# Loading PE weights once for two matmuls, and letting ACT end the kernel, in a decode step with a 64K cache

## The chip, the cores and the metric

One core of one Trainium2 chip. The metric is the device time of one execution in microseconds (us); medians of repeated executions are quoted.

Terms: PE is the matmul engine, PEld its weight loads (LDWEIGHTS), DVE the vector engine, ACT the scalar engine, POOL the general engine, SP the engine that issues most DMAs. "DMA engine" is one of the 16 that move data for a core. A "landing" is the moment at which a transfer's last data is reported. "Warm" and "cold" are PE at a granted clock of 1.00 and of 0.50.

## The reference, cut to what matters

One token (B = Sq = 1) passes through a grouped-query attention with a 65,536-position cache, and through a small gated MLP; the two are mixed by a sigmoid gate.

```python
q = (x @ wq).reshape(1, 1, 32, 128)                   # wq 1024 x 4096
scores = einsum('bhqd,bhkd->bhqk', q, k) * 128**-0.5  # 4 kv heads, 8 q heads on each
o = einsum('bhqk,bhkd->bhqd', softmax(scores), v)
a = o.reshape(1, 1, 4096) @ wo                        # wo 4096 x 1024
b = gated_mlp(x, w_in, w_sp, b_sp, w_out)             # w_in 1024 x 3584, w_out 1792 x 1024
return g * a + (1 - g) * b                            # g = sigmoid(sum(x * gate_w))
```

K and V are 64 MiB each in bf16. With the weights the kernel reads 162 MB for one token, and every byte is used once.

## The kernel before

All big inputs pass through four buffers of 32 KB per partition (4 MB each), in one queue issued by SP. A buffer is loaded again when its last reader is done.

```python
kv = ctx.enter_context(tc.tile_pool(name="kv", bufs=4))
def load(src, shape, name):
    t = kv.tile([P, CT * P], BF16, name=name, tag="kv")      # 128 partitions x 32 KB
    ...
    nc.sync.dma_start(out=v, in_=src)
```

A K tile is transposed on DVE in four quarters, and each quarter is multiplied by 128 columns that hold the queries. The two values of `k` use the same weights, but each `nc.tensor.matmul` brings its own load:

```python
for v in range(VC):                                    # VC = 4 quarters
    nc.vector.transpose(out=kt[:].bitcast(I32), in_=kb[:, v * n:(v + 1) * n])
    ...
    for b in range(BP):                                # BP = 4
        for k in range(2):
            nc.tensor.matmul(s_ps[:, k * HN:(k + 1) * HN],       # 512 columns
                lhsT=wt[g % 2][:, v, b]..., rhs=kx[:, b // 2, b % 2, ...], ...)
```

The second product (probabilities times V) uses 32 columns of the PE array at a time, so that four matmuls stand side by side in the array:

```python
for c in range(CC):                                    # CC = 32
    t = c % NB                                         # NB = 4 column groups of 32
    nc.tensor.matmul(o_ps[g][t * B:(t + 1) * B, :], lhsT=ptt[g, j][:, c, :],
                     rhs=vx[:, c], ...)                # 128 x 512
```

The end: the last tile is `wo`, in pieces of 16, 8, 4, 2, 1 and 1 rows per partition. After each piece `project` multiplies what has come, and the result goes out:

```python
nc.vector.tensor_copy(out=out_sb[:], in_=out_ps[:])
nc.sync.dma_start(out=out..., in_=out_sb[::B, :])
```

## Time and profile before

| | before |
|---|---|
| time, median (lowest to highest) | 386.87 us (386.82 to 386.92) |
| span of the profiled execution | 385.2 us |
| queue of inputs (q1) | 162.01 MB, 98.1% of the time of 16 engines |
| PE, PE loads, DVE busy | 55%, 23%, 54% |

Lines of the page of the kernel before: the span; busy us, share of the span and count of instructions of each engine; and of three DMA queues packets, MB, and the share of 16 engines' span that their packets took.

```profile
span 385.2 us, 3265 instructions
...
PE 212.4 (55%) x1396; PEld 89.7 (23%) x1396; DVE 209.2 (54%) x207; ACT 39.2 (10%) x54; POOL 4.4 (1%) x10
...
q1 hardware_dynamic: 6200, 162.01, 98.1%
q8 instruction: 11, 0.18, 0.2%
q14 instruction: 4, 0.03, 0.0%
```

The input queue fills the DMA engines; nothing else comes near. The queues q8 and q14 look like nothing: they fetch instructions, 0.2% in all.

The groups that the change is about (line, engine, operation, tiles, shapes, count | busy us, mean ns of one | idle before, releaser):

```profile
L301 PE MATMUL s_ps<-kt,wt 128*128 128x512 bf16 x512 | 139.0, 426 | 88.4 <-DVE kt L295 87.2
...
L301 PEld LDWEIGHTS <-wt 128*128 128x128 bf16 x512 | 52.6, 105 | 173.5 <-DVE kt L295 72.8
L344 PE MATMUL o_ps<-vt,pt 128*32 128x512 bf16 x512 | 39.4, 457 | 15.4 <-DMA vt<-in_A_v_cache_dram 15.4
...
L344 PEld LDWEIGHTS <-pt 128*32 128x32 bf16 x512 | 15.9, 109 | 34.9 <-issue 27.1
```

Each of the two products has 512 matmuls and 512 loads. In steady state, from the timeline (start us, duration us):

```profile
205.55 1.90 PE L301 MATMUL s_ps<-kt,wt 128*128 128x512 bf16 x8 [0.29 <-DVE kt L295]
...
207.38 1.91 PE L344 MATMUL o_ps<-vt,pt 128*32 128x512 bf16 x32
```

Eight score matmuls take 1.90 us, 0.24 us each. The 32 matmuls of a whole V tile take 1.91 us, 0.06 us each, as four run side by side. And the first half of an x projection, at the start:

```profile
12.24 3.18 PE L190 MATMUL z_ps<-win_t,xT 128*32 128x448 bf16 x32
```

The end of the chain of waits (start us, duration us, what):

```profile
347.38 34.34 DMA wo_t<-in_A_wo_dram
...
381.76 0.43 PE out_ps L382 x4
...
382.22 0.42 DVE out_sb L421
```

The last `wo` piece is issued at 347.4 us and has landed at 381.72; then come 0.43 us of matmul, 0.42 us of copy, and the store. So the kernel ends about 3.5 us after its last input byte is reported.

Windows of half a microsecond there (window, length, busy time and count of PE, PEld, DVE, ACT, POOL, the PE clock granted, DMA share, GB/s):

```profile
379.50:380.00 0.50, 0.33 (x14) 0.14 (x5) 0.00 (x0) 0.00 (x0) 0.00 (x0) 1.00 0.19 70
380.00:380.50 0.50, 0.04 (x4) 0.04 (x7) 0.00 (x0) 0.00 (x0) 0.00 (x0) 1.00 0.24 82
380.50:381.00 0.50, 0.36 (x8) 0.17 (x8) 0.00 (x0) 0.00 (x0) 0.00 (x0) 1.00 0.13 49
```

The share is 0.19, 0.24 and 0.13.

### The profile page before, as it was taken

The numbers are of one execution on the slowest core, as the hardware profiler recorded it, in microseconds if no ns is written. First come the engines' busy times: TensorE is split into PE (matmuls) and PEld (weight loads), VectorE is DVE, ScalarE is ACT, GpSimd is POOL, SyncE is SP. The second block draws the span as 40 slices with busy tenths as digits, with TensorE's granted clock in tenths as the row PEclk, the third lists the DMA queues.
The fourth block names the chain that finished last, engine by engine and source line by source line (L and its number), as shares of the span: only waits on it lengthen the run. The fifth ranks groups of instructions, "written<-read, shape, count | busy, mean of one in ns | idle before, by whom it ended". The sixth has DMA issues, their size and how long they took to land.

```text
span 385.2 us, 3265 instructions
## 1 busy us (share of the span) xinstructions
PE 212.4 (55%) x1396; PEld 89.7 (23%) x1396; DVE 209.2 (54%) x207; ACT 39.2 (10%) x54; POOL 4.4 (1%) x10
## 2 busy tenths in 40 slices
PE   0433447775377656464876474637773837663352
PEld 0111113232222212122322121222221312331141
DVE  5141288996697372757864636569646456510010
ACT  1010001111601101014011010140110101400000
POOL 4000000000000000000000000000000000000000
PEclk9966559999779969695699695977895958565558
DMA  8999999999999999999999999999999999999993
GB/s 334 429 436 434 436 433 432 436 431 435 432 429 427 429 419 434 432 432 436 434 436 429 434 429 433 422 436 427 425 432 430 436 436 436 427 429 430 427 408 149
DMA packets 6251, 162.23 MB, mean 421 GB/s; under 512 B 728, under 2 KB 732, under 8 KB 1116
## 3 DMA queue, kind: packets, MB, share of 16 engines
q1 hardware_dynamic: 6200, 162.01, 98.1%
q8 instruction: 11, 0.18, 0.2%
q14 instruction: 4, 0.03, 0.0%
q10 hardware_dynamic: 36, 0.00, 0.0%
HBM read 162.01 MB, written 0.00 MB: 421 GB/s over the span
## 4 chain that ended last, share of the span: by engine, by line
DMA 65%; DVE 18%; PE 9%; issue 5%; ACT 1%; SPq 0%; ACTq 0%; DVEq 0%
DMA kn<-in_A_k_cache_dram 44%; DVE kt L295 15%; DMA vt<-in_A_v_cache_dram 9%; DMA wo_t<-in_A_wo_dram 9%; PE s_ps L301 6%; DMA wb<-in_B_b_sp_dram 2%; DVE pt L335 1%; PE o_ps L344 1%; PE z_ps L190 1%; ACT sc L310 1%; PE om_ps L355 0%; SPq L417 0%; ACT sc L332 0%; DVE mx L314 0%; DVE mx L297 0%
## 5 line engine op out<-in xcount | busy, mean ns | idle before, releaser
L301 PE MATMUL s_ps<-kt,wt 128*128 128x512 bf16 x512 | 139.0, 426 | 88.4 <-DVE kt L295 87.2
L295 DVE STREAM_TRANSPOSE kt<-kn 128x2048 int32<-128x2048 int32 x64 | 143.3, 2283 | 68.4 <-DMA kn<-in_A_k_cache_dram 68.4
L301 PEld LDWEIGHTS <-wt 128*128 128x128 bf16 x512 | 52.6, 105 | 173.5 <-DVE kt L295 72.8
L344 PE MATMUL o_ps<-vt,pt 128*32 128x512 bf16 x512 | 39.4, 457 | 15.4 <-DMA vt<-in_A_v_cache_dram 15.4
L310 ACT CAST sc<-s_ps 128x1024 bf16<-128x1024 f32 x16 | 16.2, 1013 | 254.9 <-PE s_ps L301 254.9
L344 PEld LDWEIGHTS <-pt 128*32 128x32 bf16 x512 | 15.9, 109 | 34.9 <-issue 27.1
L335 DVE STREAM_TRANSPOSE pt<-sc 128x1024 bf16<-128x1024 bf16 x16 | 18.6, 1217 | 6.8 <-ACT sc L332 6.8
L332 ACT ACTIVATE sc<-sc,nb 128x1024 bf16<-128x1024 bf16 x16 | 18.2, 1136 | 9.5 <-DVE nb L328 9.5
L352 DVE COPY o_sb<-o_ps 128x512 f32<-128x512 f32 x4 | 2.6, 662 | 27.2 <-PE o_ps L344 27.2
L297 DVE TENSOR_REDUCE mx<-sc 128x1 f32<-128x1024 bf16 x12 | 14.3, 1188 | 1.2 <-ACT sc L310 1.1
L355 PE MATMUL om_ps<-o_sb,pick 128*32 128x128 f32 x32 | 7.7, 421 | 13.1 <-DVE o_sb L352 13.1
L190 PE MATMUL q_ps<-wq_t,xT 128*32 128x512 bf16 x64 | 7.1, 623 | 9.1 <-DMA wq_t<-in_A_wq_dram 9.1
L314 DVE TENSOR_REDUCE mx<-sc 128x1 f32<-128x1024 bf16 x4 | 4.9, 1220 | 12.3 <-ACT sc L310 12.3
L382 PE MATMUL out_ps<-wo_t,oa 128*32 128x256 bf16 x128 | 6.0, 334 | 7.7 <-DMA wo_t<-in_A_wo_dram 7.7
L190 PEld LDWEIGHTS <-xT 128*32 128x32 bf16 x128 | 5.2, 140 | 20.5 <-issue 20.5
L355 PEld LDWEIGHTS om_ps<-o_sb,pick 128*32 128x32 f32 x32 | 5.0, 168 | 17.2 <-DVE o_sb L352 16.3
L254 DVE TENSOR_TENSOR rowt<-q_ps,own_b 128x512 f32<-128x512 f32 x2 | 1.3, 685 | 14.1 <-PE q_ps L190 14.1
L190 PE MATMUL z_ps<-win_t,xT 128*32 128x448 bf16 x64 | 6.2, 567 | 4.8 <-DMA win_t<-in_B_w_in_dram 4.8
L421 DVE CAST out_sb<-out_ps 128x256 bf16<-128x256 f32 x1 | 0.4, 425 | 12.4 <-PE out_ps L382 12.4
L318 PE MATMUL mt_ps<-ident_f,m 128*1 128x128 f32 x4 | 1.2, 296 | 10.2 <-DVE m L316 10.2
L382 PEld LDWEIGHTS <-oa 128*32 128x32 bf16 x128 | 4.4, 116 | 9.1 <-issue 7.2
L202 DVE TENSOR_TENSOR rowt<-z_ps,own_b 128x448 f32<-128x448 f32 x2 | 1.2, 620 | 9.3 <-PE z_ps L190 9.3
(86 smaller groups left out, 57.4 us busy)
## 6 DMA issues: line engine op xcount, KB each, us to landing
kn<-in_A_k_cache_dram SPq DMA_DIRECT2D x16, 4096.0 KB, 27.1
vt<-in_A_v_cache_dram SPq DMA_DIRECT2D x16, 4096.0 KB, 34.6
wq_t<-in_A_wq_dram SPq DMA_DIRECT2D x2, 4096.0 KB, 28.3
win_t<-in_B_w_in_dram SPq DMA_DIRECT2D x2, 3584.0 KB, 15.0
wo_t<-in_A_wo_dram SPq DMA_DIRECT2D x1, 4096.0 KB, 31.1
wout_t<-in_B_w_out_dram SPq DMA_DIRECT2D x1, 3584.0 KB
wo_t<-in_A_wo_dram SPq DMA_DIRECT2D x1, 2048.0 KB
wo_t<-in_A_wo_dram SPq DMA_DIRECT2D x1, 1024.0 KB
```

Of the source, the lines that this page charges most:

```text
L190: nc.tensor.matmul(ps[t * B:(t + 1) * B, k * HN:k * HN + n], lhsT=xT[:, i * KH + c:i * KH + c + 1].to_broadcast([P, B]), rhs=w[:, c, o:o + ...
L295: nc.vector.transpose(out=kt[:].bitcast(I32), in_=kb[:, v * n:(v + 1) * n])
L297: nc.vector.reduce_max(**late.pop())
L301: nc.tensor.matmul(s_ps[:, k * HN:(k + 1) * HN], lhsT=wt[g % 2][:, v, b].rearrange("p a v h -> p (a v h)"), rhs=kx[:, b // 2, b % 2, k * C ...
L310: nc.scalar.copy(out=sct[g, j][:], in_=s_ps[:])
L314: nc.vector.reduce_max(**late.pop())
L332: nc.scalar.activation(out=sct[g, j][:], in_=sct[g, j][:], func=ACT.Exp, scale=SCALE, bias=nb[:, 0:1], accum_out=lss[g][:, j:j + 1])
L335: nc.vector.transpose(out=ptt[g, j][:].rearrange("p c x -> p (c x)"), in_=sct[g, j][:])
L344: nc.tensor.matmul(o_ps[g][t * B:(t + 1) * B, :], lhsT=ptt[g, j][:, c, :], rhs=vx[:, c], start=(j == 0 and c < NB), stop=(j == NT - 1 and ...
L352: nc.vector.tensor_copy(out=o_sb[:], in_=o_ps[g][:])
L355: nc.tensor.matmul(om_ps[gs, :], lhsT=pick[:, i * REP:(i + 1) * REP, :].rearrange("p h q -> p (h q)"), rhs=o_sb[:, i * DH:(i + 1) * DH], s ...
L382: nc.tensor.matmul(out_ps[t * B:(t + 1) * B, :], lhsT=vec[:, c0 + c:c0 + c + 1].to_broadcast([P, B]), rhs=w[:, c, t * NO:(t + 1) * NO], st ...
```

## The change

Its intent: take PE's repeated weight loads out. The second matmul of a pair keeps the weights of the first, and a hook deletes its LDWEIGHTS from the finished program. For the second product that means pairs of chunks as 64 columns (two matmuls with the same 64 columns; half of each result is of use), which gives a larger `o_ps` and another `head_out`. ACT does the last copy and the store.

```diff
+    def drop_repeated_loads(n):        # run on the finished program
+        ...                            # deletes the LDWEIGHTS of each matmul marked by same_weights()
+    nc.at_finalize(drop_repeated_loads)
 ...                                    # x projections: t outside, k inside
-                    nc.tensor.matmul(
+                    ins = nc.tensor.matmul(
                         ps[t * B:(t + 1) * B, k * HN:k * HN + n],
 ...
+                    if k > 0:
+                        same_weights(ins)
 ...                                    # scores: the same two lines
     def v_tile(g, j, vt):
-            o_ps[g] = pso.tile([P, VC * DH], FP32, name="o_ps")
+            o_ps[g] = pso.tile([P, 2, VC * DH], FP32, name="o_ps")
-        for c in range(CC):
-            t = c % NB
-            nc.tensor.matmul(o_ps[g][t * B:(t + 1) * B, :], lhsT=ptt[g, j][:, c, :], rhs=vx[:, c], ...)
+        for u in range(CC // 2):
+            hs = slice(u % 2 * P // 2, (u % 2 + 1) * P // 2)
+            for e in range(2):
+                ins = nc.tensor.matmul(o_ps[g][hs, e, :],
+                    lhsT=ptt[g, j][:, 2 * u:2 * u + 2, :].rearrange("p c x -> p (c x)"),
+                    rhs=vx[:, 2 * u + e], ...)
+                if e > 0:
+                    same_weights(ins)
     def head_out(g):                    # copy and 4 matmuls become a masked product, a sum and 1 matmul
 ...
-    nc.vector.tensor_copy(out=out_sb[:], in_=out_ps[:])
-    nc.sync.dma_start(out=out..., in_=out_sb[::B, :])
+    nc.scalar.copy(out=out_sb[:], in_=out_ps[:])
+    nc.scalar.dma_start(out=out..., in_=out_sb[::B, :])
```

One effect is not in the diff's lines: tiles were removed, added and resized ahead of the four big buffers, so these moved by 544 bytes in each partition (43,968 to 44,512, by the addresses in the two built programs).

More of the change, by code (lines that the diff above doesn't have):

```diff
@@ L73, with same_weights @@
     pss = ctx.enter_context(tc.tile_pool(name="pss", bufs=2, space=bass.MemoryType.PSUM))
-    psm = ctx.enter_context(tc.tile_pool(name="psm", bufs=2, space=bass.MemoryType.PSUM))
+    psm = ctx.enter_context(tc.tile_pool(name="psm", bufs=1, space=bass.MemoryType.PSUM))
     pso = ctx.enter_context(tc.tile_pool(name="pso", bufs=1, space=bass.MemoryType.PSUM))
     psl = ctx.enter_context(tc.tile_pool(name="psl", bufs=1, space=bass.MemoryType.PSUM))
+    held = set()
+    def same_weights(ins):
+        held.add(ins.ins.name)
+    def drop_repeated_loads(n):
+        for block in n.main_func.blocks:
+            drop, load_at = [], None
+            for i, ins in enumerate(block.instructions):
+                kind = type(ins).__name__
+                if kind == "InstLdweights":
+                    load_at = i if ins.sync_info is None else None
+                elif kind == "InstMatmult":
+                    if ins.name in held and load_at is not None:
+                        drop.append(load_at)
+                    load_at = None
+            for i in reversed(drop):
+                del block.instructions[i]
+    nc.at_finalize(drop_repeated_loads)
     def load(src, shape, name):
@@ L121 @@
         nc.gpsimd.memset(t[:], 0.0)
-    pbits = const.tile([P, 5], I32, name="pbits")
+    pbits = const.tile([P, 6], I32, name="pbits")
     for i, m in enumerate((P // KC - 1, B - 1, QD - 1, REP - 1)):
@@ L128 @@
                             scalar2=None, op0=ALU.logical_shift_right)
-    pf = const.tile([P, 6], FP32, name="pf")
+    nc.vector.tensor_scalar(out=pbits[:, 5:6], in0=pidx[:], scalar1=REP.bit_length() - 1,
+                            scalar2=2 * VC - 1, op0=ALU.logical_shift_right, op1=ALU.bitwise_and)
+    pf = const.tile([P, 7], FP32, name="pf")
     nc.vector.tensor_copy(out=pf[:, 0:1], in_=pidx[:])
-    nc.vector.tensor_copy(out=pf[:, 1:6], in_=pbits[:])
+    nc.vector.tensor_copy(out=pf[:, 1:7], in_=pbits[:])
     def one_hot(shape, dtype, in0, col, name):
@@ L178 @@
     nc.vector.tensor_copy(out=own_bb[:], in_=own_b[:].unsqueeze(1).to_broadcast([P, NB, B]))
-    pick = one_hot([P, B, QD], FP32, row[:, :B].unsqueeze(2).to_broadcast([P, B, QD]), 2, "pick")
+    own_8 = one_hot([P, 2 * VC], FP32, row[:, :2 * VC], 6, "own_8")
     own_q = one_hot([P, QD], FP32, row[:, :QD], 3, "own_q")
@@ L186, in x_rows @@
         for c in range(KH):
-            for k in range(F // (NB * ZN) if n == ZN else NHB):
-                for t in range(NB):
+            for t in range(NB):
+                for k in range(F // (NB * ZN) if n == ZN else NHB):
                     o = (k * NB + t) * n
-                    nc.tensor.matmul(
+                    ins = nc.tensor.matmul(
                         ps[t * B:(t + 1) * B, k * HN:k * HN + n],
@@ L300, in k_tile @@
                 for k in range(2):
-                    nc.tensor.matmul(
+                    ins = nc.tensor.matmul(
                         s_ps[:, k * HN:(k + 1) * HN],
@@ L306, in k_tile @@
                         skip_group_check=True)
+                    if k > 0:
+                        same_weights(ins)
         if j == 0:
@@ L339, in v_tile @@
         if j == 0:
-            o_ps[g] = pso.tile([P, VC * DH], FP32, name="o_ps")
+            o_ps[g] = pso.tile([P, 2, VC * DH], FP32, name="o_ps")
         vx = vt.rearrange("p (v c d) -> p c v d", v=VC, d=DH)
-        for c in range(CC):
-            t = c % NB
-            nc.tensor.matmul(
-                o_ps[g][t * B:(t + 1) * B, :], lhsT=ptt[g, j][:, c, :], rhs=vx[:, c],
-                start=(j == 0 and c < NB), stop=(j == NT - 1 and c >= CC - NB),
-                skip_group_check=True)
+        for u in range(CC // 2):
+            hs = slice(u % 2 * P // 2, (u % 2 + 1) * P // 2)
+            for e in range(2):
+                ins = nc.tensor.matmul(
+                    o_ps[g][hs, e, :],
+                    lhsT=ptt[g, j][:, 2 * u:2 * u + 2, :].rearrange("p c x -> p (c x)"),
+                    rhs=vx[:, 2 * u + e], start=(j == 0 and u < 2),
+                    stop=(j == NT - 1 and u >= CC // 2 - 2), skip_group_check=True)
+                if e > 0:
+                    same_weights(ins)
@@ L349, in head_out @@
     def head_out(g):
         gs = slice(g * B, (g + 1) * B)
-        o_sb = wk.tile([P, VC * DH], FP32, name="o_sb")
-        nc.vector.tensor_copy(out=o_sb[:], in_=o_ps[g][:])
-        om_ps = psm.tile([P, DH], FP32, name="om_ps", tag="m")
-        for i in range(VC):
-            nc.tensor.matmul(
-                om_ps[gs, :],
-                lhsT=pick[:, i * REP:(i + 1) * REP, :].rearrange("p h q -> p (h q)"),
-                rhs=o_sb[:, i * DH:(i + 1) * DH], start=(i == 0), stop=(i == VC - 1),
-                skip_group_check=True)
@@ L360, in head_out @@
-        ls_ps = psm.tile([P, NT], FP32, name="ls_ps", tag="m")
-        nc.tensor.matmul(ls_ps[gs, :], lhsT=hsel[:].rearrange("p h q -> p (h q)"),
-                         rhs=lss[g][:], start=True, stop=True, skip_group_check=True)
+        om8 = big.tile([P, 2 * VC, DH], FP32, name="om8")
+        nc.vector.tensor_tensor(
+            out=om8[:], in0=o_ps[g][:].rearrange("p e (v d) -> p (e v) d", d=DH),
+            in1=own_8[:].unsqueeze(2).to_broadcast([P, 2 * VC, DH]), op=ALU.mult)
+        o_sb = wk.tile([P, DH], FP32, name="o_sb")
@@ new lines, in head_out @@
+        nc.vector.tensor_reduce(out=o_sb[:], in_=om8[:].rearrange("p x d -> p d x"), axis=AX.X,
+                                op=ALU.add)
+        om_ps = psm.tile([P, DH + NT], FP32, name="om_ps", tag="m")
+        hs = hsel[:].rearrange("p h q -> p (h q)")
+        nc.tensor.matmul(om_ps[gs, DH:], lhsT=hs, rhs=lss[g][:], start=True, stop=True,
+                         skip_group_check=True)
+        nc.tensor.matmul(om_ps[gs, :DH], lhsT=hs, rhs=o_sb[:], start=True, stop=True,
+                         skip_group_check=True)
@@ L363, in head_out @@
         rl = wk.tile([P, 2], FP32, name="rl")
-        nc.vector.reduce_sum(out=rl[gs, 0:1], in_=ls_ps[gs, :], axis=AX.X)
+        nc.vector.reduce_sum(out=rl[gs, 0:1], in_=om_ps[gs, DH:], axis=AX.X)
         nc.vector.reciprocal(out=rl[gs, 1:2], in_=rl[gs, 0:1])
@@ L367, in head_out @@
         nc.vector.tensor_tensor(
-            out=om[gs], in0=om_ps[gs, :].rearrange("p (q c) -> p q c", c=OC),
+            out=om[gs], in0=om_ps[gs, :DH].rearrange("p (q c) -> p q c", c=OC),
             in1=own_q[gs, :].unsqueeze(2).to_broadcast([B, QD, OC]), op=ALU.mult)
@@ L420 @@
     out_sb = const.tile([P, NO], BF16, name="out_sb")
-    nc.vector.tensor_copy(out=out_sb[:], in_=out_ps[:])
-    nc.sync.dma_start(out=out.rearrange("o t (q n) -> (o t q) n", n=NO), in_=out_sb[::B, :])
+    nc.scalar.copy(out=out_sb[:], in_=out_ps[:])
+    nc.scalar.dma_start(out=out.rearrange("o t (q n) -> (o t q) n", n=NO), in_=out_sb[::B, :])
     last = {}
```

## The prediction

> **What bounds the kernel.** The input stream. The DMA queue table gives 162.01 MB in queue q1, whose packets fill 98.1% of the 16 engines' span; the slice row stays near 427 to 436 GB/s. The Trainium skill ("DMA: Bandwidth & Descriptors", Specifications) names 435 GB/s as the fabric ceiling; this trace agrees (436 in the best slices). 162.01 MB at the middle's 431 GB/s is 376 of 385.2 us (estimate). The rest is about 2.5 us before the first bytes and 5 us after the stream thins out (in the windows the DMA share falls to 0.2 at 379.5 us). PE is busy 55%, its loads 23%, DVE 54%. By the issue times against bytes moved, the queue always holds 9 to 35 us of issued work, least near 115 us: a buffer freed a few us earlier or later changes nothing.
>
> **What the change does.**
> 1. Scores: 256 of 512 loads go. A warm quarter of a K tile (8 matmuls) takes 1.90 us; I guess 0.22 to 0.23 per matmul after, for 0.24. PE busy there falls from 139 to 125–135 us. The quarters are paced by the 2.28 us transposes on DVE, these by the DMA: off the path.
> 2. Second product: before, four 32-column matmuls run side by side (32 in 1.91 us warm, 3.60 cold). After, 64 columns leave two places, and the two matmuls of a pair use the same one, so on average two run at once: 3.8 us warm, 5.5–7 cold (estimate, double). Loads fall from 512 to 256, but matmul busy rises from 39 to about 75 us: worse for PE. There is room: a K and V pair costs PE about 10 + 3.8 us, and its stream takes 19.4.
> 3. x projections: also two side by side instead of four; a half goes from 3.0–3.6 to 5.5–7 us. The q chain starts 2–3 us later; the first K transpose (50.9 us) slips by 0.5–2 us. The backlog absorbs it.
> 4. head_out: a 0.69 us copy and 1.9 us of matmuls become two DVE operations of about 1.2 us (estimate from the 128x1024 reduction, 1.22 us) and 0.5 us of matmul: +0.3 us.
> 5. End: ACT copies (about 0.38 us, estimate from 1013 ns for 1024 columns and 171 ns for one) where DVE took 0.425, and issues the store itself: 0.1 us and one hop saved.
>
> **On the critical path.** Only 5, and perhaps 2 and 4 in the tail. The last V tile lands at 362.08 us; oa was ready at 369.8, the first wo tile lands at 371.8. After: oa at 372–373, some us later if the pairs do not overlap. The projection of the first wo tile (3.2 us) then ends near 376, before the second wo piece (376.7), and even a few us more are caught up before the last piece at 381.7, which still ends the kernel.
>
> **Predicted:** 386.6 us, 80% range 386.0 to 387.2. Faster by over 2%: 0.01; within 2%: 0.97; slower by over 2%: 0.02.
>
> **What would show it.** Queue share near 98%, mean about 421 GB/s; loads fall from 1396 to about 800, their busy time to about half; o_ps matmul busy nearly doubles (last V tile 5.5–7 us); DVE waits longer for kn; the last wo piece lands near 381.7; the chain of waits is still mostly DMA.
>
> **What would make it wrong.** Pairs that do not overlap, so that head_out ends after 376 us and the catch-up fails (up to +2 us); a starved queue near 115 us, seen as a slice clearly below 420 GB/s; a slow start of the store on ACT (+0.3 us); a DMA rate that shifts with the buffers' places.

## The result and the profile after

| | before | after |
|---|---|---|
| time, median of 4 runs | 386.89 us | 385.80 us (385.71 to 385.88) |
| span of the profiled execution | 385.2 us | 383.9 us |
| last `wo` piece landed | 381.72 us | 380.64 us |
| instruction fetches on q8 | 11 | 8 |

The ratio is 0.9971 (95% interval 0.9953 to 0.9988). Ratios here are the mean time of one kernel's fast runs over that of the other's of the same rounds, so they are not quite the ratios of the medians. The gain is 1.1 us where 0.3 was predicted, and the time lies below the stated range.

The page after:

```profile
span 383.9 us, 2650 instructions
...
PE 242.3 (63%) x1372; PEld 59.3 (15%) x796; DVE 218.5 (57%) x211; ACT 39.6 (10%) x55; POOL 4.4 (1%) x10
...
q1 hardware_dynamic: 6192, 162.01, 98.5%
q8 instruction: 8, 0.13, 0.1%
```

The loads fall to 796 and PEld from 89.7 to 59.3 us. PE busy rises. The bytes are the same. q8 has 8 fetches for 11. The groups of the two products in the changed kernel (256 loads each, for 512):

```profile
L326 PE MATMUL s_ps<-kt,wt 128*128 128x512 bf16 x512 | 142.3, 437 | 67.9 <-DVE kt L320 67.3
...
L372 PE MATMUL o_ps<-vt,pt 128*64 128x512 bf16 x512 | 69.2, 432 | 8.8 <-DMA vt<-in_A_v_cache_dram 8.8
L326 PEld LDWEIGHTS <-wt 128*128 128x128 bf16 x256 | 27.6, 108 | 184.0 <-issue 122.9
...
L372 PEld LDWEIGHTS <-pt 128*64 128x64 bf16 x256 | 17.2, 124 | 57.9 <-issue 56.4
```

The same eight score matmuls and the same V tile in the timeline of the changed kernel:

```profile
205.67 1.89 PE L326 MATMUL s_ps<-kt,wt 128*128 128x512 bf16 x8 [0.30 <-DVE kt L320]
...
207.49 3.65 PE L372 MATMUL o_ps<-vt,pt 128*64 128x512 bf16 x32
```

And its first half projection, with k inside and t outside:

```profile
12.30 3.18 PE L213 MATMUL z_ps<-win_t,xT 128*32 128x448 bf16 x32
```

Eight score matmuls take 1.89 us with half of their loads gone, for 1.90: the loads had been hidden. A V tile takes 3.65 us instead of 1.91: with 64 columns only two matmuls run side by side. For PE the change is a loss. The half projection takes 3.18 us in either order.

The end of its chain of waits:

```profile
349.05 31.60 DMA wo_t<-in_A_wo_dram
...
380.69 0.32 PE out_ps L414 x4
...
381.02 0.37 ACT out_sb L453
```

And its windows of half a microsecond:

```profile
379.50:380.00 0.50, 0.27 (x8) 0.07 (x1) 0.00 (x0) 0.00 (x0) 0.00 (x0) 1.00 0.45 168
380.00:380.50 0.50, 0.29 (x4) 0.10 (x4) 0.00 (x0) 0.00 (x0) 0.00 (x0) 1.00 0.04 12
380.50:381.00 0.50, 0.29 (x4) 0.10 (x3) 0.00 (x0) 0.00 (x0) 0.00 (x0) 1.00 0.00 0
```

In the same windows the share is 0.45 and then 0.04 and 0: more engines work at 379.5 us than before, and by 380.5 all are done.

From the landing of the last piece to the end of the span it is now 3.28 us (383.92 - 380.64, the span with two decimals), for 3.45 before (385.17 - 381.72): 0.17 us less, with the shorter last matmul group (0.32 us for 0.43, at a granted clock of 1.00 in the last window shown; before, it was 0.67 from 381 to 382 us) and ACT's copy (0.37 for 0.42). The other 1.08 us lie ahead of the landing: the same 162.01 MB arrived earlier. No step of the prediction had a reason for that.

### Where the 1.08 us are: the slowest of 16 DMA engines

Each DMA raises its semaphore sixteen times, and the trace has the time of each increment. These are the sixteen of the last `wo` piece, worked out from the semaphore records, sorted:

```
before  378.35 378.38 378.42 378.44 378.63 378.92 379.02 | 379.82 379.84 380.01 380.01 380.10 380.15 380.24 | 381.52 381.72
after   378.64 378.65 378.76 378.78 379.10 379.25 379.39 | 380.09 380.27 380.34 380.34 380.46 380.47 380.48 380.63 380.64
```

The engines do not run level, though each has a sixteenth of the transfer: they come in groups some 1.5 us apart, and before, two engines come after all others. In the changed kernel these two are gone, and the rest is a little later than before, not earlier.

The DMA packets' records show what makes the groups. A 4 MB tile is 128 packets of 32 KB, eight in a row on each engine. Packets that follow each other within a few ns can be strung into one engine's stream (the strings can swap between engines in nearly equal phase, so I use them locally). One such stream in the changed kernel:

```
start us  end us  ns      bytes
102.34    103.55  1216    32768   input
103.55    104.66  1107    16384   instruction fetch (q8)
104.64    106.32  1681    32768   input
106.32    107.53  1215    32768   input
```

A 16 KB instruction fetch stops one engine's input for 1.09 us, and the packet after it takes 0.47 us more than the others: 1.55 us in all, for that engine alone. Worked out in the same way, every such fetch of the two kernels took 1.40 to 1.56 us, most of them 1.55. In both kernels each q8 fetch is followed by one such long packet, as long as the stream runs in packets of that size. The input is complete when the slowest engine is. So the time depends on how many fetches fall on the worst engine, which a share averaged over 16 engines cannot show.

The Trainium skill ("Runtime: NRT & Kernel Launch", Instruction fetch mechanics) says that instructions are fetched in blocks of 16 KiB, 256 instructions, and calls the cost of crossing a block boundary "mostly hidden". The block size agrees (q8 packets of 16,384 bytes, 11 of them for the 2,792 matmuls and loads that the page counts before, 8 for the 2,168 after). Whether PE ever waited for a fetch was not looked at; from the DMA stream the cost is not hidden.

**Theory (fetches).** The change shortens PE's instruction stream by some 620 instructions; there are 8 fetches instead of 11, no engine gets two, and the input ends earlier. **Rivals:** ACT at the end; fewer loads for PE to execute; the new order or PE's warm clock at the end; the moved buffers.

### The profile page after: what moved, and what is told of

It reads as the page before. It is cut to its first block, busy times and chain, and to the rows that moved or that the text cites. A ratio compares the mean times of both kernels' runs of the same rounds, so it can differ in the third digit from the quotient of the medians.

```text
span 383.9 us, 2650 instructions
## 1 busy us (share of the span) xinstructions
PE 242.3 (63%) x1372; PEld 59.3 (15%) x796; DVE 218.5 (57%) x211; ACT 39.6 (10%) x55; POOL 4.4 (1%) x10
## 3 DMA queue, kind: packets, MB, share of 16 engines
q1 hardware_dynamic: 6192, 162.01, 98.5%
HBM read 162.01 MB, written 0.00 MB: 422 GB/s over the span
## 4 chain that ended last, share of the span: by engine, by line
DMA 60%; DVE 20%; PE 11%; issue 5%; ACT 2%; SPq 1%; DVEq 0%; ACTq 0%
DMA kn<-in_A_k_cache_dram 47%; DVE kt L320 16%; DMA wo_t<-in_A_wo_dram 8%; PE s_ps L326 8%; DMA win_t<-in_B_w_in_dram 5%; DVE pt L362 2%; PE o_ps L372 2%; ACT sc L337 1%; PE z_ps L213 1%; ACT sc L359 1%; DVE mx L341 1%; DVE o_sb L387 0%; SPq L449 0%; ACT L359 0%; PE nb_ps L352 0%
## 5 line engine op out<-in xcount | busy, mean ns | idle before, releaser
L326 PE MATMUL s_ps<-kt,wt 128*128 128x512 bf16 x512 | 142.3, 437 | 67.9 <-DVE kt L320 67.3
L372 PE MATMUL o_ps<-vt,pt 128*64 128x512 bf16 x512 | 69.2, 432 | 8.8 <-DMA vt<-in_A_v_cache_dram 8.8
L326 PEld LDWEIGHTS <-wt 128*128 128x128 bf16 x256 | 27.6, 108 | 184.0 <-issue 122.9
L372 PEld LDWEIGHTS <-pt 128*64 128x64 bf16 x256 | 17.2, 124 | 57.9 <-issue 56.4
L383 DVE TENSOR_TENSOR om<-o_ps,own 128x1024 f32<-128x1024 f32 x4 | 4.8, 1205 | 26.8 <-PE o_ps L372 26.8
L393 PE MATMUL om_ps<-o_sb,hsel 128*32 128x128 f32 x8 | 2.4, 398 | 13.6 <-DVE o_sb L387 13.6
L387 DVE TENSOR_REDUCE o_sb<-om 128x128 f32<-128x1024 f32 x4 | 7.5, 1871 | 0.1
L213 PEld LDWEIGHTS <-xT 128*32 128x32 bf16 x64 | 3.0, 140 | 20.3 <-issue 20.3
```

The lines of the kernel that those rows point to most:

```text
L213: ins = nc.tensor.matmul(ps[t * B:(t + 1) * B, k * HN:k * HN + n], lhsT=xT[:, i * KH + c:i * KH + c + 1].to_broadcast([P, B]), rhs=w[:, c, ...
L326: ins = nc.tensor.matmul(s_ps[:, k * HN:(k + 1) * HN], lhsT=wt[g % 2][:, v, b].rearrange("p a v h -> p (a v h)"), rhs=kx[:, b // 2, b % 2, ...
L372: ins = nc.tensor.matmul(o_ps[g][hs, e, :], lhsT=ptt[g, j][:, 2 * u:2 * u + 2, :].rearrange("p c x -> p (c x)"), rhs=vx[:, 2 * u + e], sta ...
L383: nc.vector.tensor_tensor(out=om8[:], in0=o_ps[g][:].rearrange("p e (v d) -> p (e v) d", d=DH), in1=own_8[:].unsqueeze(2).to_broadcast([P, ...
L387: nc.vector.tensor_reduce(out=o_sb[:], in_=om8[:].rearrange("p x d -> p d x"), axis=AX.X, op=ALU.add)
```

## The experiments

All 11 gave correct results and ran beside the kernel before on the same chip; its medians there were 386.88 to 386.99 us. "Last" is the last increment of the last piece in the profiled execution.

| run | q8 fetches | median us | ratio to before | last, us |
|---|---|---|---|---|
| before | 11 | 386.87 | 1 | 381.72 |
| after | 8 | 385.80 | 0.9971 | 380.64 |
| e1_act_end | 11 | 386.71 | 0.9998 | 381.51 |
| e2_keep_loads | 11 | 387.23 | 1.0009 | 382.04 |
| e3_drop_scores | 10 | 386.74 | 0.9996 | 381.73 |
| e4_pool_fill | 8 | 385.66 | 0.9968 | 380.74 |
| e5_after_aligned | 8 | 383.92 | 0.9924 | 378.70 |
| e6_before_aligned | 11 | 385.26 | 0.9958 | 380.06 |
| e7_fill14 | 14 | 387.26 | 1.0010 | 382.15 |
| e8_fill18 | 18 | 388.65 | 1.0045 | 383.64 |
| e9_after_at448 | 8 | 385.51 | 0.9960 | 380.48 |
| e10_after_at128 | 8 | 385.44 | 0.9959 | 380.32 |
| e11_after_at256 | 8 | 383.91 | 0.9924 | 378.72 |

### e1: only the end on ACT

```diff
-    nc.vector.tensor_copy(out=out_sb[:], in_=out_ps[:])
-    nc.sync.dma_start(out=out..., in_=out_sb[::B, :])
+    nc.scalar.copy(out=out_sb[:], in_=out_ps[:])
+    nc.scalar.dma_start(out=out..., in_=out_sb[::B, :])
```

> The kernel before with only the end moved to ACT (copy and store). Fetch theory (the stream ends earlier after the change because fewer 16 KB instruction fetches on queue q8 interrupt the DMA engines, and the slowest engine had two such fetches before and one after): the fetches stay 11, the last wo piece still lands near 381.7 us in the trace, and the time falls by 0.0 to 0.2 us only. Rival (the end on ACT is the gain): about 385.8 us, -1.1 us.

386.71 us, ratio 0.9998 (0.9985 to 1.0010): no change that the runs can tell. By the interval it is at most 0.6 us, where the rival needed 1.1. The end on ACT is not the gain.

### e2: the change with its repeated loads kept

```diff
-    nc.at_finalize(drop_repeated_loads)
```

> The changed kernel with the repeated loads kept in the program (576 PE instructions more, all else as changed: order of matmuls, pairs of 64 columns, head_out, ACT end). Fetch theory: q8 fetches go from 8 to 10 or 11, some engine gets two, the last wo piece lands near 381.7 us, and the time is 386.4 to 387.0 us, 0.2 below the kernel before at most by its end on ACT. Rivals (new order of the matmuls, PE pace or warm clock at the end, new places of the buffers): stays at 385.8 us, within 0.2.

The line of q8 in its DMA table:

```profile
q8 instruction: 11, 0.18, 0.2%
```

The gain is gone: 387.23 us, ratio 1.0009, and the last increments are `... 380.52 380.52 380.53 | 381.87 382.04`: two late engines again. Everything else of the change is still there: order, pairs, buffers, `head_out`, ACT. So the loads taken out are worth 1.40 us in the last increment (382.04 - 380.64), the whole gain and a little more. The run is 0.2 us above the expected range; with the loads kept, the change is not 0.2 us below the kernel before but slightly above it. e5 to e11 find out why.

It does not yet say whether the loads count as PE work or as instructions. The next runs do.

### e3: only the score loads dropped, from the kernel before

The hook and `same_weights` of the change, for the scores alone (256 loads less).

> The kernel before with only the 256 repeated loads of the scores taken out: no other change of order, buffers or end. Fetch theory: one q8 fetch fewer (10 for 11); if still two of them fall on one engine the time stays within 0.2 us of 386.9, if not it falls by about 1 us to 385.9; the spread of the sixteen increments of the last piece must say the same as the time (last minus first about 3.3 us, or about 2 us). Rival (PE work itself counts): a fall in proportion to the loads taken out, -0.5 us, with the spread unchanged.

386.74 us, ratio 0.9996 (0.9983 to 1.0008). 256 loads fewer on PE, 24 us less of PEld, 10 fetches instead of 11, and no gain. The last increments are `... 380.26 380.29 380.41 | 381.73`: one late engine instead of two. Two or one, the slowest decides. The time alone does not exclude the 0.5 us that the rival expected (the interval reaches down to -0.66 us); the last increment does not move, and this speaks against PE's work and against a cost in proportion to instructions. e7 and e8 decide it.

### e4: 768 tiny instructions on POOL, in the changed kernel

```diff
+    fill = const.tile([1, 8], FP32, name="fill")
+    ...                                  # before each of the 16 K tiles:
+        nc.gpsimd.memset(fill[:], 0.0)   # 48 times
```

> The changed kernel with 768 tiny memsets of one scratch tile added on the idle POOL engine (48 KB of instructions); nothing waits for them. Fetch theory: some 3 to 6 more instruction fetches in the DMA table, a wider spread of the last piece's increments, time up by 0.5 to 1.5 us to 386.3 to 387.3. Rivals in which PE's work, the order, the buffers or the end made the gain: no change, 385.8 us within 0.2.

The number missed: 385.66 us, no slower than the changed kernel. The DMA table has the expected fetches, six more of 8 KB on q14:

```profile
q8 instruction: 8, 0.13, 0.1%
q14 instruction: 10, 0.08, 0.1%
```

The increments show two things at once:

```
after  378.64 378.65 378.76 378.78 379.10 379.25 379.39 380.09 380.27 380.34 380.34 380.46 380.47 380.48 380.63 | 380.64
e4     377.14 377.19 377.31 377.48 377.72 377.73 378.44 378.45 378.55 378.61 378.62 378.64 378.69 378.73 378.78 | 380.74
```

One engine is 2 us behind all others: the strings of packets put all six added fetches on one engine. The sizes fit: an added fetch and the longer packet after it take about 0.62 us of their engine (measured on four of the six), so six take 3.7, and the last engine is 3.4 us behind the early group, which has lost one member (six for seven). That is the fetch theory, though not spread over engines as I had thought. But the 15 others are about 1.5 us earlier than in the changed kernel, which no fetch can explain. The packets themselves were shorter: 1213.0 ns for 32 KB, for 1217.9 in the changed kernel. The added tile of 32 bytes had moved the four big buffers to a multiple of 512 bytes. So e4 was two experiments in one, and the next two separate them.

### e5 and e6: the buffers at a multiple of 512 bytes

In the changed kernel (e5), ahead of the big buffers; in the kernel before (e6) the same with 16 columns, 64 bytes:

```diff
+    pad = const.tile([P, 8], FP32, name="pad")       # 32 bytes in each partition
+    nc.gpsimd.memset(pad[:], 0.0)
```

> The changed kernel with 32 bytes of padding ahead of the big buffers, so that the four K/V buffers start at a multiple of 512 bytes in each partition (they start 480 bytes past one in the changed kernel, 448 past one in the kernel before). Placement theory (read from e4, whose scratch tile of 32 bytes happened to do the same: its 32 KB packets took 1213.0 ns, for 1217.6 in the changed kernel): packets 1213.0 ns, 8 fetches on q8, first of the sixteen last increments near 377.1 us, last near 379.0, time 384.0 to 384.5 us. Rival (e4's short packets came from the POOL instructions or from chance): packets 1217.6 ns and 385.8 us.

> The kernel before with 64 bytes of padding, K/V buffers at a multiple of 512 bytes; program otherwise untouched, 11 fetches. Placement and fetches add up: packets 1213.0 ns for 1216.5, about 310 packets to an engine, so 1.1 to 1.3 us less: 385.6 to 385.9 us; two engines with two fetches still late, last increments 3 us apart. If placement does nothing by itself: 386.9 us.

e5: 383.92 us, ratio 0.9924 (0.9911 to 0.9936). e6: 385.26 us, ratio 0.9958. Packets take 1213.0 ns in both. Both runs are a little faster than expected (384.0 to 384.5 and 385.6 to 385.9). Both theories hold, and they add up: between e6 and e5 lie 1.36 us in the last increment (380.06 - 378.70), much as the 1.40 of e2. One reason why e6 gained more than expected shows in the packets: a fetch took 1.41 us of its engine there (one 1.27), for 1.55, and the slowest engine has two.

The DMA table and the end of the chain of e5, to compare with those of the changed kernel:

```profile
DMA packets 6248, 162.18 MB, mean 425 GB/s; under 512 B 728, under 2 KB 732, under 8 KB 1116
...
q8 instruction: 8, 0.13, 0.1%
```

```profile
347.38 31.32 DMA wo_t<-in_A_wo_dram
...
378.74 0.32 PE out_ps L416 x4
```

The last piece lands at 378.70 us, 1.94 earlier than in the changed kernel, and all that follows takes as long as there. Most of the 1.94 us is in the packets: the time of all q1 packets, divided by 16 engines, fell from 377.97 to 376.47 us.

### e7 and e8: more PE instructions, to see steps

From e2, with one-column weight loads ahead of each quarter's score matmuls, 14 (e7) or 30 (e8) at a time; the result stays correct, as every matmul there loads its own weights after them.

```diff
+            for _ in range(14):                     # e8: 30
+                nc.tensor.ldweights(xT[:, 0:1])
```

> e2 (changed kernel, repeated loads kept, 11 fetches) with 896 one-column weight loads added on PE in the score tiles: about 14 fetches. The lanes of e2 and of the kernel before suggest that PE's fetches go round eight DMA engines, so that the 9th and 10th fall on the engines of the 1st and 2nd. Then 9 to 16 fetches in the stream all leave two on the worst engine, and the time is that of e2, 387.2 us within 0.3; last increments spread by about 3.3 us but more of them late (5 or 6 instead of 2). Rival (each PE instruction or each fetch costs its share): +0.5 to +1 us.

> As e7 with 1920 added loads, about 18 fetches. Rotation over eight: the 17th falls on an engine that has two already, so the worst has three, spread of the last increments about 4.8 us and time 1.2 to 1.6 us above e7: 388.4 to 388.9. Rival with an even cost per instruction: about twice the step from e2 to e7.

e7: 387.26 us. 896 instructions and three fetches more than e2, and 0.03 us of difference (they ran on two chips; the ratios to the kernel before, 1.0009 and 1.0010, say the same). e8: 388.65 us, 1.39 us above e7. Both as the fetch theory expected.

The line of q8 in e8's DMA table, and the last increments of e2, e7 and e8:

```profile
q8 instruction: 18, 0.29, 0.3%
```

```
e2  378.61 378.73 378.86 379.19 379.25 379.26 379.60 | 380.21 380.38 380.39 380.48 380.52 380.52 380.53 | 381.87 382.04
e7  378.58 378.63 378.66 379.01 379.08 379.31 379.39 | 380.16 380.58 380.58 | 381.81 381.97 382.05 382.05 382.09 382.15
e8  378.64 378.69 378.77 378.80 379.22 379.34 379.37 | 380.63 | 381.61 381.82 381.90 381.99 382.03 382.07 | 383.58 383.64
```

The same seven early increments in all three: engines without a q8 fetch. The other nine move up by groups. If PE's fetches go round eight engines, then with ten of them inside the stream (e2) two engines have two; with fourteen (e7) six have two; with eighteen (e8) six have two and two have three. Those are just the sizes of the late groups, and the ninth late engine, at 380.1 to 380.6 in all three, is one with two of the 8 KB fetches of q14 in the strings. So the time is a staircase: the fetches beyond 8 cost about 1.4 us, those beyond 16 as much again, and in between they are free. The strings agree: in e8, fetches 1, 9 and 17 fall on one engine. Over a whole run strings can swap, so they were made once more: all packets were matched at once by the usual gaps between followers (3 or 4 ns of overlap, or 2 or 3 ns of pause). In e8, fetches n and n + 8 then share a string for every n from 1 to 10; in e7 for n from 1 to 5, but not for 6. A cost for each instruction would have put e7 well above e2.

### e9, e10, e11: which placement counts

The padding of e5 with 480, 160 and 288 bytes: buffers 448, 128 and 256 bytes past a multiple of 512.

> The changed kernel with its K/V buffers where the kernel before has them, 448 bytes past a multiple of 512 (192 past one of 256). The placement theory, with an offset theory in it: the packet time depends on the offset alone, so 1216.8 ns in the body of the stream for 1217.8, and 385.4 to 385.6 us, which takes the new placement's cost of about 0.3 us out of the change. If the packets stay at 1217.8 ns, the two kernels' packets differ for another reason.

> As e5, buffers 128 bytes past a multiple of 512 (and of 256). If a multiple of 128 is enough, packets take 1213.0 ns and the time is 383.9 us as in e5; if a multiple of 256 is needed, packets take 1215 to 1218 ns and the time is 384.7 to 385.8.

> As e5, buffers 256 bytes past a multiple of 512. If a multiple of 256 is enough, 1213.0 ns and 383.9 us as in e5; if 512 is needed, 1215 to 1218 ns and 384.7 to 385.8 us.

Mean time of the 32 KB input packets between 50 and 350 us, without the one after each fetch, against the offset past a multiple of 256 bytes:

| kernel | offset, bytes | packet, ns | median us |
|---|---|---|---|
| e5, e11 | 0 | 1213.0 | 383.92, 383.91 |
| e10 | 128 | 1216.8 | 385.44 |
| e9 | 192 | 1216.8 | 385.51 |
| after | 224 | 1217.9 | 385.80 |
| before (11 fetches) | 192 | 1216.8 | 386.87 |

A multiple of 256 is enough, and 128 is not. The Trainium skill ("DMA: Bandwidth & Descriptors", How a descriptor splits into AXI transactions) has the same boundary: descriptors are split at 256 B, and one that does not start there costs more. The page says this of the side that is read; what moved here is the buffer that is written. The boundary agrees; the extra time did not grow evenly with the offset (3.8 ns at 128 and at 192, 4.9 at 224).

With the buffers where the kernel before has them, the changed kernel runs at 385.51 us (e9): by moving them, the change had lost about 0.3 us of what it won. The estimate from the packets is the same: 280 packets of 32 KB on each engine (4,480 over 16), each 1.1 ns longer, give 0.31 us. And before to e2 it is 0.32 us in the last increment. (The last increment of e9 itself is only 0.16 us earlier than that of the changed kernel; its profiled run was its slowest, 385.69 us.)

e5 is the best version, with e11 equal to it: 383.92 us, 2.9 us below the kernel before and 1.9 below the changed one.

## Why the prediction was right or wrong

**Right: the bound, and that PE does not matter.** The kernel is bound by its input stream; the change is within 2%. Score loads: 256 off the path, as said. Pairs of 64 columns: 3.65 us for a V tile, predicted 3.8; 5.33 us for the last one, predicted 5.5 to 7 for a cold one (its granted clock averaged 0.68, where it had been 0.50 before); `o_ps` busy 69.2 us, predicted about 75. The later `oa` (1.7 us) was caught up before the last piece, and the input queue never ran dry.

**Wrong in size or kind, without effect on the time.** I guessed that a score matmul would fall from 0.24 to 0.22 or 0.23 us without its load; it stayed at 0.24 (1.89 us for eight). I said that the x projections would double, as a pair uses the same column group; they did not change (3.18 us). The Trainium skill ("TensorEngine Tiling (Array Packing)", Key Properties) says that tiles operate independently, and the trace agrees: the matmuls of the other column groups did not wait behind a pair. `head_out`'s sum over a strided view took 1.87 us, not 1.2.

**The step that failed.** The prediction was 386.6 us with a range from 386.0; the time was 385.80. In the prediction's words: "Only 5, and perhaps 2 and 4 in the tail" lie on the critical path, and "the last piece at 381.7 ... still ends the kernel". It landed at 380.64. The step took the stream's time as bytes over a rate common to all engines, so that in its sum nothing moved the last landing (a starved queue and a rate that shifts with the buffers' places were named as risks). The runs showed three terms in place of one:

| term | predicted us | measured us | shown by |
|---|---|---|---|
| fewer instruction fetches, worst engine from two to one | 0 | -1.40 | e2 against after; steps in e7 and e8 |
| buffers moved from 192 to 224 past a multiple of 256 | 0 (named as a risk) | +0.32 | before against e2; e9 |
| after the last landing (ACT, PE's clock) | -0.1 and a hop | -0.17 | profiles; e1 bounds the ACT part |

The sum is -1.25 us, the difference of the two profiled spans (383.92 - 385.17); the medians differ by 1.09, as the profiled run of the kernel before was slower than its median (387.03 us) and that of the changed kernel faster (385.71). Each term rests on single profiled executions and can be off by 0.1 to 0.2 us. That the change came out faster, as predicted, was luck: what was to make it faster, the end, gave at most 0.17 us, and the rest came from a term that the prediction did not have. The mistake in reading was to dismiss q8 because its share was 0.2%. A share of 16 engines is an average; 0.2% of 16 engines' span is about 12 us of one engine.

**What stays open.** That the fetches go round eight engines is inferred from the group sizes and from strings of packets; the records do not name engines. A step of the staircase is 1.36 us in the last increment with aligned buffers (e6 to e5), near the 1.41 of a fetch there; without, it is 1.40 and 1.49 (e2 to the changed kernel, e7 to e8), somewhat below the 1.55 of a fetch, and why was not looked into. Why POOL's fetches all fall on one engine was not tried. The packets of `wq` (20 to 38 us) took 1213.0 ns in the kernel before although their buffers have the same offset as K's; so the offset is not the whole rule, and what else enters was not tested.

## What to carry to other kernels

When a kernel is bound by one stream over all DMA engines, look at when each engine finishes its part of the last transfer, not at the mean share. Count PE's instructions in blocks of 256 (POOL's came in 8 KB, 128 of its 768 added instructions to a fetch): here a shorter program paid through the DMA engines and not through PE, and only where it crossed a step (8 or 16 fetches while the stream runs; the last fetch of the kernel before fell on an engine that was done). Place the buffers of such a stream at a multiple of 256 bytes: 32 bytes of padding gained more here than the whole change.

## What the Trainium skill lacked or had wrong

- "Runtime: NRT & Kernel Launch", Instruction fetch mechanics: calls the cost of a block boundary "mostly hidden". Here each 16 KB fetch took about 1.55 us from one DMA engine (1.41 with the buffers at a multiple of 256 bytes), and the fetches beyond the 8th, and again beyond the 16th, cost the kernel about 1.4 us (e7 to e8: 387.26 to 388.65). The page doesn't say what a fetch costs the data on the same DMA engines, nor how fetches are spread (by inference: PE's over eight engines, POOL's six on one).
- "DMA: Bandwidth & Descriptors", How a descriptor splits into AXI transactions: gives the 256 B boundary, but not what it costs a large load with an unaligned SBUF side. Here 3.8 to 4.9 ns on 1213 ns for 32 KB, and 1.5 to 1.9 us of the kernel (e5 against e10 and after).
- The same page, Where 436 GB/s comes from: says that for HBM to SBUF the HBM side (about 358 GB/s) binds, without saying there that this needs more than one busy core; the same paragraph recalls a measured 425 GB/s. This case, with one core busy, reads HBM at 419 to 425 GB/s over the whole span (e8 and e5).
- No page that I read says to compare the sixteen increments of one DMA: they spread over 3.4 us before (378.35 to 381.72), under a queue share of 98.1%.
